# New opening order, one-operation end decays and a split last tile in a planned attention + MLP kernel

## The chip, the cores and the metric

One core of one Trainium2 chip runs the kernel. Its engines, each with a queue of its own that is worked through strictly in order: PE (TensorE, matrix products), DVE (VectorE), ACT (ScalarE, with function tables that must be loaded), POOL (GpSimd) and SP (SyncE, which here issues nearly all DMAs). The metric is the device time of one launch in microseconds (us); lower is better. A time of this kernel is told apart from no change when it moves by more than about 1%.

## The reference

The inputs are four batches of 8 heads, 768 tokens and head size 48. Three stages follow one another; everything is float32.

```python
# 1. linear attention with a decay per key channel
f = 1 / (1 + exp(-f_logit))
for t in range(S):
    state = f[:, :, t, :, None] * state + k_t (outer) v_t
    y[:, :, t] = q_t @ state
# 2. spatial gating MLP on x = y, (tokens, 384)
h = gelu_tanh(x @ w_in); u, v = halves of h
v_s = w_sg @ (normalised v * g_ln) + b_sg      # mixes tokens
x = x + (u * v_s) @ w_out
# 3. token and channel mixing
theta = x @ w_theta
y = w_tok_r @ (x * cos(theta)) + w_tok_i @ (x * sin(theta))
u = x + y;  out = u + relu(u @ w_ch)
```

## The kernel before

**Units.** A batch is worked in two halves of 384 tokens. In a half, the 8 heads lie in four pairs; the fourth pair's channels are packed into free rows of the first three pairs' tiles and are moved to their place by small DMAs (L801, two per pair). The attention of one pair and half is a *unit*: three transposes of K on PE (L822), a copy of them on ACT (`kt`, L826), state updates (L834) and scores (L843) on PE, the mask on DVE (`am`, L855), six small state steps on DVE (L871 to L880) with decays on ACT (L885), then the products inside the chunk (L925) and the carried-in products (L980 in batch 0), a copy of the result on ACT (`y`, L911), and DMAs that bring `y` into the activations `xst` (L902).

**Preparing a half** (`half`, `scaled`). The logits are loaded (L705), turned into decays (ACT L726 and L727), scanned on DVE (L735; its seeds come from a POOL memset L725 and a DVE step L730), inverted by Ln and Exp on ACT (L738, L739), and then K and Q are multiplied by them on DVE (L778 to L781). The decays at the chunk ends are made by two DVE operations of 128x3 (L785, L786) into `bends`, and ACT copies them into the tile (L789). For the fourth pair POOL clears a tile (L709).

**The order of the carried-in products** in batch 0 (`apart`). Their first product needs a signal that the products inside the chunk have ended in PSUM. Before the change ACT copies one state block over a part of `am` that those products read (L972), so that the copy has to wait for them, and the first carried-in product (L980) waits for the copy.

**Batch 0's MLP.** `w_in` arrives as 64-bit numbers and is decoded: 12 loads (L522), each with one ACT step (L534) and three DVE steps (L535 to L537) of 128x256. The v products (L1014, `mm<-early,xst`, 18 of 128x512) and the u products (L1014, `mm<-xst,early`, 128x384) read it as float32, at four passes each. ACT then makes gelu and the statistics (L1204 to L1234), and the W_sg products (L1002 to L1004, three of split float32 each) follow. Batches 1 to 3 go on in the same way with split weights, their attention laid between products of the batch before. The third stage is worked for two batches at a time (`pair`); `p7` is the last product, its DVE step L1167 and the store of the output L1171.

**What sets the order.** A planner (`Plan.schedule`) holds every operation with a length, dependencies and a due time. It picks greedily per engine and writes one fixed order per queue. Where PE would stand still in the first 100 us of its plan, it inserts warm-up products of an identity matrix (`idle`, L1382, 128x128, float32, so two records each in the trace). Numbers such as `HF0`, `V_AT`, `EVEN`, `ODD` and `RE_IN` are due times of stages. Table loads on ACT are inserted where the function in the plan changes (L346).

```python
if o.eng == "PE" and self.idle and t < WARM_TO and self.quiet(free["PE"]) is not None:   # L298
...
rate = c if ticks.get(i - 1, 0) >= 3060 else c / 2   # L254, the plan's speed of PE
```

The same program has a branch for inputs whose decays are too small (`general`); it is not run here.

Of the kernel before, what the change touches and what calls it, by code (L numbers as in the profile page):

```python
# [58 lines left out]
N_MIX, N_LMM, N_LST, N_LFM, N_LTMP = 3, 1, 5, 2, 1  # L59
EVEN, ODD = (0.05, 0.5), (0.9, 0.4)  # L60
GROUPS0 = [(p, p + 1) for p in range(NT)]
GROUPS1 = GROUPS0
LEAD = 3.0
LATE = 75.0
HF0, HF1, V_AT, U_AT, DENSE = (-60.0, -38.0), (-44.0, -16.0), -46.0, -24.0, -35.0
ATT_FROM = 0.0
ATT_TO = 100.0
PACE = 1.0
YQ = "SP"
MQ = "SP"  # L70
LOOK = 0.05
RE_IN = 4.0
SWITCH = 2.0
# [3 lines left out]

TICK = 10.24 / 3
DMA_SLACK = 1.0
BACKLOG = 2.5  # L80
# [59 lines left out]
class Plan:  # L140
# [63 lines left out]
    def schedule(self):  # L204
        for o in reversed(self.ops):
            cost = LAT[o.eng] + o.dur + ((ISSUED + LANDED + o.dma / RATE) * DMA_SLACK if o.dma else 0.0)
            for d in o.succ:
                o.vt = min(o.vt, d.vt - cost)
        free = {e: 0.0 for e in LAT}
        ticks = {}  # L210
        cand = {e: [] for e in LAT}
# [38 lines left out]
        def run(a, dur, left):  # L250

            c, i = left / dur, int(a / TICK + 1e-9)
            while left > 1e-6:
                rate = c if ticks.get(i - 1, 0) >= 3060 else c / 2  # L254
                n = min(left, rate * ((i + 1) * TICK - a))
                ticks[i] = ticks.get(i, 0) + n
                left, a, i = left - n, a + n / rate, i + 1
            return a
# [99 lines left out]
def body(tc, ctx, att, lat, qkv, flog, w_in, g_ln, w_sgT, b_sg, w_out, w_theta, w_rT, w_iT, w_ch, out):  # L358
# [36 lines left out]

    gate = const.tile([P, 1], F32, name="gate")
    halfpi = fill("halfpi", math.pi / 2)
    mhalf = fill("mhalf", -0.5, NS)
# [112 lines left out]
    def a1(n):  # L511
        return 0.1 + n * 0.00081
# [156 lines left out]

    first, ends = Buf(), []  # L670

# [11 lines left out]
    def half(pl, g, b, hf, xst, carry, vt, step):  # L683
# [14 lines left out]
        qk, parts = [], []  # L698
        later = [first] if b else []
        for p, (t, root) in enumerate(tiles):  # L700
            for p0, p1 in groups:
                if p0 == p:
                    dma(
                        pl, eng, P * (p1 - p0) * TH * 4,
                        lambda gp=slice(p0, p1): q[eng].dma_start(f.t[:, gp], flog[b, hf][:, gp]), later, wp=fp[p0:p1],  # L705
                    )
            if p == NT:
                moved, vb, clear = (Buf(of=root) for _ in range(3))
                pl.op("POOL", 0.1 + QKE * 0.0008, lambda t=t: nc.gpsimd.memset(t.t[:, :QKE], 0.0), w=[clear], vt=vt)  # L709
                dma(pl, eng, P * VAL * 4, lambda t=t, p=p: q[eng].dma_start(t.t[:, QKE:], qkv[b, p, hf][:, QKE:]), later, wp=[vb])  # L710
                part = [moved, moved, vb, clear]
            else:
                part = [Buf(of=root) for _ in range(4)]
                dma(pl, eng, P * QKV * 4, lambda t=t, p=p: q[eng].dma_start(t.t, qkv[b, p, hf]), later, wp=part)
            qk.append(t)
            parts.append(part)
# [49 lines left out]
    def scaled(pl, b, hf, p, f, fb, seed, sb, be, bb, t, parts, t3, parts3):  # L766
# [9 lines left out]
        if b == 0:  # L776
# [28 lines left out]
    def unit(pl, g, b, hf, p, be, bb, t, parts, xst, carry):  # L805
# [42 lines left out]
        if before:  # L848
            r, w, dur, fn = before
            pl.op("PE", 0.25 + 0.1 * nu + dur - 0.12, lambda fn=fn: (fn(), scores()), r=[kb, qb, vb, kt, *r], w=[ps, *w], small=True)  # L850
# [79 lines left out]
        if fused:  # L930
# [27 lines left out]
            if hf == 1 and p == NP - 1:  # L958
                r, w, dur, fn = both_
                pl.op("PE", dur, fn, r=r, w=w, small=True)  # L960
                out2()
            else:
                carry["last"], carry["out"] = both_, out2
            return

        def apart():
            pl.op("PE", 0.5, inner, r=[vb, am], w=[ps], small=True)
            late = range(1 - hf, 2 * NC2)
            turn = [(c, j) for c in late for j in range(2)]
            c0 = late[0]  # L970
            behind = lambda: am.t[wide[1], 1, (NC2 - 1) * HP : (NC2 - 1) * HP + D]
            pl.op("ACT", 0.2, lambda: nc.scalar.copy(behind()[:D], S[c0][0]()[rows[1]]), r=[S[c0][1]], w=[am])  # L972
            turn.remove((c0, 1))
            turn.insert(0, (c0, 1))

            def carried():
                for c, j in turn:
                    i, a = halves[c]
                    moved = (c, j) == turn[0]
                    nc.tensor.matmul(  # L980
                        score(a, i)[rows[j]], behind()[:D] if moved else S[c][0]()[rows[j]], Q()[rows[j], tok(i, a)], start=False,
                        stop=i == NC2 - 1,
                    )

            pl.op("PE", 0.134 * len(late), carried, r=[qb, *(S[c][1] for c in late), am], w=[ps], small=True)
            output()
# [4 lines left out]
    def moe(pl, g, xst, get, wmid, out_b, pace, first=False):  # L991
# [164 lines left out]

        def p7(hf, w):
# [112 lines left out]

    def pair(pl, g, batches, sets, get, ws, between=None):

# [99 lines left out]
        use(1)  # L1372
        p7b(0, ws[1])

# [10 lines left out]
    with tc.manual_schedule():  # L1385
# [76 lines left out]
        pair(pl, g, [blocks(b, again(b))[2] for b in (1, 2)], more, get, mids)  # L1462
        pl.emit()
# [153 lines left out]
```

## Time and profile before

| | |
|---|---|
| median of 3 runs | 595.15 us (592.37 to 598.02) |
| the profiled execution | 594.94 us, span 593.2 us |
| PE busy | 572.7 us (97% of the span) |
| DVE, ACT, POOL busy | 473.8, 374.0, 24.8 us |
| granted TensorE clock, mean | 0.998 |
| DMA | 136.26 MB, 230 GB/s on average |

The span is what the profile sees; the execution's own time is 1.7 us longer. PE is busy nearly all the time, but that counts warm-up products too, and the share is an average: from 14 to 36 us DVE has almost no idle time, from 43 to 78 us ACT has almost none, and after that PE works nearly without a pause to 586.9 us. The chain that ended last names for each stretch the engine whose work ended the wait.

### The profile page before, as it was taken

The numbers are of one execution on the slowest core, as the hardware profiler recorded it, in microseconds if no ns is written. First come the engines' busy times: TensorE is split into PE (matmuls) and PEld (weight loads), VectorE is DVE, ScalarE is ACT, GpSimd is POOL, SyncE is SP. The second block draws the span as 40 slices with busy tenths as digits, with TensorE's granted clock in tenths as the row PEclk, the third lists the DMA queues.
The fourth block names the chain that finished last, engine by engine and source line by source line (L and its number), as shares of the span: only waits on it lengthen the run. The fifth ranks groups of instructions, "written<-read, shape, count | busy, mean of one in ns | idle before, by whom it ended". The sixth has DMA issues, their size and how long they took to land.

```text
span 593.2 us, 14971 instructions
## 1 busy us (share of the span) xinstructions
PE 572.7 (97%) x5767; PEld 528.7 (89%) x5767; DVE 473.8 (80%) x1127; ACT 374.0 (63%) x828; POOL 24.8 (4%) x38
## 2 busy tenths in 40 slices
PE   8889999989999999999999999999999999999995
PEld 8646687978799989999999998999999999999995
DVE  5987789999789998699886777999968459898542
ACT  5869998569795668957488335785344249553410
POOL 3002000011001010000000000000000000000000
PEclk9999999999999999999999999999999999999999
DMA  8669574878787799787899898366788745548612
GB/s 284 177 190 306 190 216 139 283 221 251 233 278 255 255 286 329 229 247 208 275 319 328 286 330 310 125 211 231 247 273 265 249 142 158 162 135 252 187 41 85
DMA packets 61295, 136.26 MB, mean 230 GB/s; under 512 B 8096, under 2 KB 28320, under 8 KB 61216
## 3 DMA queue, kind: packets, MB, share of 16 engines
q1 hardware_dynamic: 61216, 135.23, 70.5%
q8 instruction: 47, 0.77, 0.6%
q14 instruction: 32, 0.26, 0.1%
HBM read 93.90 MB, written 34.21 MB: 216 GB/s over the span
## 4 chain that ended last, share of the span: by engine, by line
PE 72%; DVE 11%; ACT 8%; DMA 5%; issue 2%; SPq 1%; POOL 0%; DVEq 0%; ACTq 0%; POOLq 0%
PE mm L1002 16%; PE mm L1004 15%; PE mm L1003 15%; PE lmm L1004 5%; PE lmm L1002 5%; PE lmm L1003 5%; PE mm L1382 2%; DMA xst<-y 2%; PE at L940 2%; ACT L346 2%; PE at L925 1%; PE at L843 1%; PE at L822 1%; PE at L834 1%; DVE tmp L1083 1%
## 5 line engine op out<-in xcount | busy, mean ns | idle before, releaser
L1002 PE MATMUL mm<-st,ar 128*128 128x384 f32 x192 | 67.0, 349 | 0.9 <-ACT tmp L1204 0.6
L1004 PE MATMUL mm<-st,ar 128*128 128x384 f32 x192 | 64.5, 336 | 0.2 <-DVE ar L1238 0.2
L1003 PE MATMUL mm<-st,ar 128*128 128x384 f32 x192 | 64.2, 334 | 0.0
L1036 ACT CAST early<-xst 128x384 fp32r<-128x384 f32 x42 | 21.4, 511 | 30.6 <-DVE xst L1041 23.2
L1002 PEld LDWEIGHTS mm<-st,ar 128*128 128x128 f32 x192 | 36.0, 188 | 2.8 <-ACT tmp L1204 0.9
L1296 ACT CAST wout<-ar 128x384 fp32r<-128x384 f32 x48 | 24.2, 511 | 19.5 <-PE lmm L1003 9.6
L1004 PEld LDWEIGHTS mm<-st,ar 128*128 128x128 f32 x192 | 36.0, 188 | 0.5 <-DVE ar L1238 0.5
L1003 PEld LDWEIGHTS mm<-st,ar 128*128 128x128 f32 x192 | 36.1, 188 | 0.4 <-issue 0.2
L1002 PE MATMUL mm<-ar,wout 128*128 128x384 f32 x96 | 33.7, 351 | 1.7 <-DVE tmp L1128 1.3
L1002 PE MATMUL mm<-early,win 128*128 128x384 f32 x102 | 35.1, 345 | 0.0
L1004 PE MATMUL mm<-early,win 128*128 128x384 f32 x102 | 34.2, 336 | 0.0
L1003 PE MATMUL mm<-early,win 128*128 128x384 f32 x102 | 34.2, 335 | 0.0
L1003 PE MATMUL mm<-ar,wout 128*128 128x384 f32 x96 | 32.5, 338 | 0.9 <-DVE ar L1025 0.9
L1004 PE MATMUL mm<-ar,wout 128*128 128x384 f32 x96 | 32.2, 336 | 0.0
L1297 DVE TENSOR_TENSOR wout<-ar,wout 128x384 fp32r<-128x384 f32 x48 | 25.5, 551 | 7.3 <-ACT wout L1296 7.2
L1002 PE MATMUL mm<-win,early 128*128 128x512 f32 (+1 forms) x78 | 30.8, 394 | 0.0
L1004 PE MATMUL mm<-win,early 128*128 128x512 f32 (+1 forms) x78 | 29.4, 376 | 0.3 <-DVE early L1037 0.3
L1003 PE MATMUL mm<-win,early 128*128 128x512 f32 (+1 forms) x78 | 29.3, 375 | 0.0
L1041 DVE TENSOR_TENSOR xst<-xst,mm 128x384 f32<-128x384 f32 x42 | 22.5, 548 | 7.9 <-PE mm L1004 7.7
L346 ACT ACT_TABLE_LOAD x19 | 24.4, 1283 | 1.1 <-PEq L1609 0.8
L1041 DVE TENSOR_TENSOR xst<-xst,lmm 128x384 f32<-128x384 f32 x30 | 15.7, 549 | 11.8 <-PE lmm L1004 11.8
L1037 DVE TENSOR_TENSOR early<-xst,early 128x384 fp32r<-128x384 f32 x42 | 22.4, 551 | 2.2 <-ACT early L1036 2.1
(304 smaller groups left out, 1812.8 us busy)
## 6 DMA issues: line engine op xcount, KB each, us to landing
st<-scratch SPq DMA_DIRECT2D x76, 384.0 KB, 4.0
scratch<-wt SPq DMA_DIRECT2D x48, 384.0 KB, 4.1
lst<-scratch SPq DMA_DIRECT2D x44, 384.0 KB, 3.8
qkv<-in_qkv SPq DMA_DIRECT2D x21, 538.0 KB, 5.6
scratch<-st SPq DMA_DIRECT2D x12, 384.0 KB, 3.6
raw<-in_w_rT SPq DMA_DIRECT2D x12, 384.0 KB, 6.0
raw<-in_w_iT SPq DMA_DIRECT2D x12, 384.0 KB, 5.3
out<-xst SPq DMA_DIRECT2D x24, 192.0 KB, 2.2
```

What stands on the lines that cost most here:

```text
L346: self.nc.scalar.preload_act_table_set(SETS[load])
L822: nc.tensor.transpose(ps.t[:, 0, c], K()[:, c], ident)
L940: nc.tensor.matmul(o[rows[j]], state_[rows[j]], Q()[rows[j], tok(i, a)], start=False, stop=i == NC2 - 1 and a == 1,)
L1002: nc.tensor.matmul(o, h0, h1, start=start, stop=False, skip_group_check=more)
L1003: nc.tensor.matmul(o, h0, l1, start=False, stop=False, skip_group_check=more)
L1004: nc.tensor.matmul(o, l0, h1, start=False, stop=stop, skip_group_check=more)
L1036: pl.op("ACT", a1(TH), lambda: nc.scalar.copy(Xh(), T()), [src], [hi])
L1037: pl.op("DVE", v1(TH), lambda: V.tensor_sub(Xl(), T(), Xh().bitcast(F32)), [src, hi], [lo])
L1041: pl.op("DVE", v1(TH), lambda: V.tensor_add(T(), T(), ps.t[:, :TH]), [ps], [xst[hf].parts[k]])
L1296: pl.op("ACT", a1(TH), lambda: nc.scalar.copy(f.t[:, 0], st()), [sb], [hi])
L1297: pl.op("DVE", v1(TH), lambda: V.tensor_sub(f.t[:, 1], st(), f.t[:, 0].bitcast(F32)), [sb, hi], [lo])
L1382: nc.tensor.matmul(g.mm.tiles[i][:, :P], ident, ident, start=True, stop=True)
```

## The change

Six things change.

1. The planner is told other numbers: PE's work starts at 0.8 us in the plan (`PE_FROM`), the plan's first two ticks count PE at half speed (`COLD`), and five due times or spreads move (`ODD`, `HF0`, `V_AT`, `RE_IN`; `F_FIRST` is new).
2. The logits of the first two pairs are loaded before the first Q, K, V tile.
3. The clearing of the fourth pair's tiles and the seeds of half 1 wait for a small POOL copy (`opened`), which itself waits for the first scan.
4. The end decays of batch 0 are one DVE operation into the tile, and two ACT multiplications by -1 (to `bends`, and in place).
5. In `apart` the ACT copy into `am` is gone; a `drain` on PE stands ahead of the carried-in products.
6. The very last 384-column tile of the output is finished and stored in two halves, the second store from ACT's queue.

```diff
-EVEN, ODD = (0.05, 0.5), (0.9, 0.4)
+EVEN, ODD = (0.05, 0.5), (0.8, 0.6)
-HF0, HF1, V_AT, U_AT, DENSE = (-60.0, -38.0), (-44.0, -16.0), -46.0, -24.0, -35.0
+HF0, HF1, V_AT, U_AT, DENSE = (-58.0, -36.0), (-44.0, -16.0), -41.0, -24.0, -35.0
+F_FIRST = 2
-RE_IN = 4.0
+RE_IN = 2.0
+COLD, PE_FROM = 2, 0.8
...
+        free["PE"] = PE_FROM
...
-                rate = c if ticks.get(i - 1, 0) >= 3060 else c / 2
+                rate = c if i >= COLD and ticks.get(i - 1, 0) >= 3060 else c / 2
...
+        def clearing(t, clear, r=()):
+            pl.op("POOL", 0.1 + QKE * 0.0008, lambda: nc.gpsimd.memset(t.t[:, :QKE], 0.0), r, [clear], vt=vt)
...
+        if opening:
+            for i, (p0, p1) in enumerate(groups[:F_FIRST]):
+                loads(p0, p1, -200.0 + i)
...
-                pl.op("POOL", 0.1 + QKE * 0.0008, lambda t=t: nc.gpsimd.memset(t.t[:, :QKE], 0.0), w=[clear], vt=vt)
+                if not opening:
+                    clearing(t, clear, [go] if b == 0 else ())
...
-                pl.op("POOL", 0.1 + n * 0.0008, lambda gp=gp: nc.gpsimd.memset(seed.t[:, gp], 2.0**62), w=ss)
+                pl.op("POOL", 0.1 + n * 0.0008, lambda gp=gp: nc.gpsimd.memset(seed.t[:, gp], 2.0**62), [go] if hf else (), ss)
...
+                if opening and p0 == 0:
+                    pl.op("POOL", 0.1, lambda: nc.gpsimd.tensor_copy(opened, f.t[:, 0, TH - 1 :]), [fs[0]], [go])
+                    clearing(qk[NT], parts[NT][3], [go])
...
+            pl.op(
+                "DVE", 0.17, lambda: V.scalar_tensor_tensor(E(), ends(f), -2.0, ends(seed), ALU.add, ALU.mult), r=[fb, sb], w=[eb]
+            )
             def bends_():
-                V.tensor_scalar(be, ends(f), -1.0, 2.0, ALU.mult, ALU.add)
-                V.tensor_mul(be, be, ends(seed))
-            pl.op("DVE", 0.2, bends_, r=[fb, sb], w=[bb])
-            pl.op("ACT", 0.2, lambda: nc.scalar.copy(E(), be), r=[bb], w=[eb])
+                nc.scalar.mul(be, E(), -1.0)
+                nc.scalar.mul(E(), E(), -1.0)
+            pl.op("ACT", 0.4, bends_, w=[eb, bb])
...
-            pl.op("ACT", 0.2, lambda: nc.scalar.copy(behind()[:D], S[c0][0]()[rows[1]]), r=[S[c0][1]], w=[am])
...
             def carried():
-                for c, j in turn:
+                nc.tensor.drain()
+                for c in late:
...
+                if final and c == NK - 1:
+                    for i, eng in enumerate(("SP", "ACT")):
+                        h, ob = slice(i * TH // 2, (i + 1) * TH // 2), Buf()
+                        pl.op(
+                            "DVE", v1(TH // 2),
+                            lambda T=T, ps=ps, h=h: V.scalar_tensor_tensor(T()[:, h], ps.t[:, h], 0.0, T()[:, h], ALU.max, ALU.add), [ps, part], [ob],
+                        )
+                        dma(
+                            pl, eng, P * TH * 2,
+                            lambda T=T, cc=cc, h=h, eng=eng: q[eng].dma_start(out_b[cc, hf * TH + h.start : hf * TH + h.stop], T()[:, h]), [ob],
+                        )
+                    continue
```

What that does to the fixed orders, at three places. Lines in the changed file are shifted by 3 to 24.

PE, the start (`mm` from `ident` are warm-up products, `at` a unit's PSUM tile, `qkv` its tile); before:

```order
L1382 MATMUL mm_103<-ident 128x128 x26
L822 MATMUL at_107<-ident,qkv_116 128x128 x3
L1382 MATMUL mm_103<-ident 128x128 x13
L834 MATMUL at_107<-qkv_116,kt_180 64x48 x12
L843 MATMUL at_107<-qkv_116 64x64 x12
```

and now:

```order
L1406 MATMUL mm_104<-ident 128x128 x17
L840 MATMUL at_108<-ident,qkv_119 128x128 x3
L1406 MATMUL mm_104<-ident 128x128 x13
L852 MATMUL at_108<-qkv_119,kt_169 64x48 x12
L861 MATMUL at_108<-qkv_119 64x64 x12
```

Nine of 26 warm-up products ahead of the first transposes are gone; the 13 behind them stay.

PE again, from the third unit of half 0 (before) and the fourth (now) on, where the first v products stand (`early` is the decoded `w_in`, `ar_0` holds half 1's tiles); before:

```order
L925 MATMUL at_107<-am_445,qkv_131 64x64 x12
L1014 MATMUL mm_103<-early_249,xst_0_381 128x512
L980 MATMUL at_107<-qkv_131,am_445 48x64
L980 MATMUL at_107<-qkv_131,s_443 48x64 x9
L1014 MATMUL mm_104<-early_249,xst_0_381 128x512
L1014 MATMUL mm_105<-early_249,xst_0_381 128x512
L1382 MATMUL mm_106<-ident 128x128 x2
L822 MATMUL at_107<-ident,ar_0_331 128x128 x3
L925 MATMUL at_108<-am_557,qkv_133 64x64 x12
L1382 MATMUL mm_106<-ident 128x128
L1014 MATMUL mm_103<-early_249,xst_0_381 128x512
L980 MATMUL at_108<-qkv_133,am_557 48x64
```

and now:

```order
L943 MATMUL at_109<-am_509,qkv_134 64x64 x12
L852 MATMUL at_108<-ar_0_176,kt_546 64x48 x10
L861 MATMUL at_108<-ar_0_176 64x64 x12
L993 MATMUL at_109<-qkv_134,s_506 48x64 x10
L1406 MATMUL mm_104<-ident 128x128 x6
L943 MATMUL at_108<-am_611,ar_0_176 64x64 x12
L993 MATMUL at_108<-ar_0_176,carry_296 48x64 x2
L993 MATMUL at_108<-ar_0_176,s_609 48x64 x10
L840 MATMUL at_109<-ident,ar_0_176 128x128 x3
L1026 MATMUL mm_104<-early_388,xst_0_354 128x512 x2
L852 MATMUL at_109<-ar_0_176,kt_684 64x48 x10
L861 MATMUL at_109<-ar_0_176 64x64 x12
```

The v products, which stood from the third unit on, now stand behind five whole units and the transposes of the sixth; a product that needs a later part of `xst` no longer stands ahead of the fourth unit's carried-in products.

ACT, batch 1's first half (`f`, `seed` and `qkv` are its tiles, `u` a gelu of batch 0); before:

```order
L911 COPY y_1020<-at_108 128x2x3x64
L346 ACT_TABLE_LOAD
L756 ACTIVATE seed_353<-f_817 128x1152
L346 ACT_TABLE_LOAD
L1065 ACTIVATE u_1037<-mm_105 128x384
L346 ACT_TABLE_LOAD
L757 ACTIVATE seed_353<-seed_353 128x1152
L346 ACT_TABLE_LOAD
L1204 ACTIVATE tmp_1054,stat_752<-mm_106 128x512
```

and now:

```order
L929 COPY y_1028<-at_109 128x2x3x64
L349 ACT_TABLE_LOAD
L771 ACTIVATE seed_336<-f_858 128x1152
L770 COPY bends<-f_858 128x9
L772 ACTIVATE seed_336<-seed_336 128x1152
L349 ACT_TABLE_LOAD
L1077 ACTIVATE u_1051<-mm_106 128x384
```

Two of four table loads are gone here, since Ln and Exp of the decays stand together; elsewhere in the part that runs their number is the same. On SP, six of the `w_in` loads stood ahead of the first small moves (L801) and now all 12 stand behind half 1's logits and tiles. From the third stage on the orders of the two kernels are alike but for a few rows.

## Rows read from the trace of the kernel before

**Rows 1.** The page, part 4: the chain that ended last, shares by engine.

```profile
PE 72%; DVE 11%; ACT 8%; DMA 5%; issue 2%; SPq 1%; POOL 0%; DVEq 0%; ACTq 0%; POOLq 0%
```

**Rows 2.** Busy time by stretch: from:to, length, each engine, clock, DMA share.

```profile
0.00:28.00 28.00, 24.17 (x427) 22.30 (x427) 21.07 (x73) 20.54 (x54) 6.21 (x18) 1.00 0.72 227
0.00:68.15 68.15, 61.59 (x935) 43.91 (x936) 51.85 (x162) 54.56 (x130) 9.51 (x21) 1.00 0.74 237
68.15:77.75 9.60, 8.70 (x92) 7.58 (x90) 5.22 (x11) 9.54 (x23) 1.92 (x2) 1.00 0.35 130
77.75:586.95 509.20, 502.38 (x4741) 477.23 (x4741) 416.13 (x953) 309.92 (x677) 13.39 (x15) 1.00 0.72 233
```

**Rows 3.** The same, L1382 alone (warm-up products): PE, weight loads, clock, DMA.

```profile
2.00:4.00 2.00, 2.00 (x11) 2.00 (x11) 1.00 0.96 294
8.00:10.00 2.00, 2.00 (x21) 2.00 (x19) 1.00 1.03 333
0.00:28.00 28.00, 16.84 (x110) 15.54 (x110) 1.00 0.72 227
0.00:68.15 68.15, 17.93 (x116) 16.44 (x116) 1.00 0.74 237
```

**Rows 4.** Timeline of PE, the first row: start, us, engine, line, operation, [idle before].

```profile
1.60 8.64 PE L1382 MATMUL mm<-ident 128*128 128x128 f32 x52 [1.60 <-POOL ident masks.py:199]
```

**Rows 5.** Timeline of DVE, 4 to 15 us, and one row at 46 us.

```profile
4.50 0.75 DVE L730 TENSOR_SCALAR seed<-f 128x3 f32<-128x3 f32 x1 [3.45 <-ACT f L727]
...
6.78 0.17 DVE L730 TENSOR_SCALAR seed<-f 128x3 f32<-128x3 f32 x1 [0.54 <-ACT f L727]
...
8.83 0.55 DVE L779 TENSOR_TENSOR f<-f,seed 128x384 f32<-128x384 f32 x1
9.30 0.95 DVE L735 TENSOR_TENSOR_SCAN f<-f,seed 128x384 f32<-128x384 f32 x1
10.17 0.53 DVE L781 SCALAR_TENSOR_TENSOR qkv<-f,qkv 128x384 f32<-128x384 f32 x1
...
12.10 0.56 DVE L780 TENSOR_TENSOR qkv<-qkv,seed 128x384 f32<-128x384 f32 x1 [0.65 <-ACT seed L739]
...
14.40 0.21 DVE L871 COPY s<-at 128x48 f32<-128x48 f32 x1 [1.27 <-PE at L843]
...
45.85 0.75 DVE L536 SCALAR_TENSOR_TENSOR early<-st,early 128x256 int32<-128x256 int32 x2
```

**Rows 6.** Timeline of POOL: the clearing of one tile, and the gate copy.

```profile
4.49 0.74 POOL L709 MEMSET ar<- 128x772 f32 x1
...
45.59 1.73 POOL L1395 COPY gate<-early 128x1 f32<-128x1 f32 x1 [25.34 <-DVE early L537]
```

**Rows 7.** Busy time of 14.40 to 35.90 us: PE, weight loads, DVE, ACT, POOL.

```profile
14.40:35.90 21.50, 16.89 (x357) 13.01 (x357) 21.36 (x75) 17.21 (x50) 1.06 (x1) 1.00 0.70 200
```

**Rows 8.** Timeline, 33 to 37 us: the end of half 0's fourth unit.

```profile
33.84 0.44 ACT L534 ACTIVATE early<-raw 128x256 f32<-128x256 f32 x1 [1.57 <-DMA raw<-in_w_in]
...
35.77 1.10 PE L1014 MATMUL mm<-early,xst 128*128 128x512 f32 x2 [2.38 <-DMA xst<-y]
...
36.80 0.25 PE L980 MATMUL at<-qkv,am 48*48 48x64 f32 x1
```

**Rows 9.** Timeline of ACT: the first gelu table, and two of the loads between.

```profile
43.10 1.28 ACT L346 ACT_TABLE_LOAD   x1
...
64.60 1.28 ACT L346 ACT_TABLE_LOAD   x1
...
66.40 1.28 ACT L346 ACT_TABLE_LOAD   x1
```

**Rows 10.** DMA issues by kind: count, KB each, median us from issue to landing.

```profile
st<-in_w_in SPq DMA_DIRECT2D x5, 256.0 KB, 4.7
tmp<-in_w_in SPq DMA_DIRECT2D x4, 256.0 KB, 7.2
```

**Rows 11.** Timeline of DVE: the last operation of the span.

```profile
586.95 0.56 DVE L1167 SCALAR_TENSOR_TENSOR xst<-mm,xst 128x384 f32<-128x384 f32 x1 [1.00 <-PE mm L1004]
```

More of the change, by code (lines that the diff above doesn't have):

```diff
@@ L396, in body @@
     gate = const.tile([P, 1], F32, name="gate")
+    opened = const.tile([P, 1], F32, name="opened")
     halfpi = fill("halfpi", math.pi / 2)
@@ L668, in attention @@
         return xst
-    first, ends = Buf(), []
+    first, go, ends = Buf(), Buf(), []
     def verdict(pl, g):
@@ L699, in half, with loads @@
         later = [first] if b else []
-        for p, (t, root) in enumerate(tiles):
[L701 to L706, printed above, removed]
+        def clearing(t, clear, r=()):
+            pl.op("POOL", 0.1 + QKE * 0.0008, lambda: nc.gpsimd.memset(t.t[:, :QKE], 0.0), r, [clear], vt=vt)
+        def loads(p0, p1, vt=None):
+            dma(pl, eng, P * (p1 - p0) * TH * 4, lambda: q[eng].dma_start(f.t[:, p0:p1], flog[b, hf][:, p0:p1]), later, wp=fp[p0:p1], vt=vt)
+        opening = b == 0 and hf == 0
+        if opening:
+            for i, (p0, p1) in enumerate(groups[:F_FIRST]):
+                loads(p0, p1, -200.0 + i)
+        for p, (t, root) in enumerate(tiles):
+            for i, (p0, p1) in enumerate(groups):
+                if p0 == p and not (opening and i < F_FIRST):
+                    loads(p0, p1)
             if p == NT:
                 moved, vb, clear = (Buf(of=root) for _ in range(3))
-                pl.op("POOL", 0.1 + QKE * 0.0008, lambda t=t: nc.gpsimd.memset(t.t[:, :QKE], 0.0), w=[clear], vt=vt)
+                if not opening:
+                    clearing(t, clear, [go] if b == 0 else ())
                 dma(pl, eng, P * VAL * 4, lambda t=t, p=p: q[eng].dma_start(t.t[:, QKE:], qkv[b, p, hf][:, QKE:]), later, wp=[vb])
@@ L849, in unit @@
             r, w, dur, fn = before
-            pl.op("PE", 0.25 + 0.1 * nu + dur - 0.12, lambda fn=fn: (fn(), scores()), r=[kb, qb, vb, kt, *r], w=[ps, *w], small=True)
+            pl.op("PE", 0.25 + 0.1 * nu + dur - 0.32, lambda fn=fn: (fn(), scores()), r=[kb, qb, vb, kt, *r], w=[ps, *w], small=True)
             carry.pop("out")()
@@ L959, in unit @@
                 r, w, dur, fn = both_
-                pl.op("PE", dur, fn, r=r, w=w, small=True)
+                pl.op("PE", dur - 0.26, fn, r=r, w=w, small=True)
                 out2()
@@ L968, in apart @@
             late = range(1 - hf, 2 * NC2)
-            turn = [(c, j) for c in late for j in range(2)]
-            c0 = late[0]
-            behind = lambda: am.t[wide[1], 1, (NC2 - 1) * HP : (NC2 - 1) * HP + D]
-            pl.op("ACT", 0.2, lambda: nc.scalar.copy(behind()[:D], S[c0][0]()[rows[1]]), r=[S[c0][1]], w=[am])
-            turn.remove((c0, 1))
-            turn.insert(0, (c0, 1))
             def carried():
-                for c, j in turn:
+                nc.tensor.drain()
+                for c in late:
                     i, a = halves[c]
[L979 to L985, printed above, removed]
+                    for j in range(2):
+                        nc.tensor.matmul(
+                            score(a, i)[rows[j]], S[c][0]()[rows[j]], Q()[rows[j], tok(i, a)], start=False, stop=i == NC2 - 1
+                        )
+            pl.op("PE", 0.134 * len(late) + 0.29, carried, r=[qb, *(S[c][1] for c in late)], w=[ps], small=True)
             output()
@@ L1155, in p6, with p7 @@
                 residual(pss[c], hf, c)
-        def p7(hf, w):
+        def p7(hf, w, final=False):
             for c in range(NK):
@@ L1164, in p7 @@
                 part = xst[hf].parts[c]
+                if final and c == NK - 1:
[8 more added lines that the diff above has]
+                            lambda T=T, cc=cc, h=h, eng=eng: q[eng].dma_start(out_b[cc, hf * TH + h.start : hf * TH + h.stop], T()[:, h]), [ob],
+                        )
+                    continue
                 pl.op(
@@ L1269, in moe, with pair @@
         return block1, block2, (xsplits, theta, residual, p7, mm3)
-    def pair(pl, g, batches, sets, get, ws, between=None):
+    def pair(pl, g, batches, sets, get, ws, between=None, end=False):
         V = nc.vector
@@ L1372, in pair @@
         use(1)
-        p7b(0, ws[1])
+        p7b(0, ws[1], end)
     pl = Plan(nc)
@@ L1461, in body @@
             more.append((Cells(bufs), [[[Buf(of=h) for _ in range(2)] for _ in range(NK)] for h in bufs]))
-        pair(pl, g, [blocks(b, again(b))[2] for b in (1, 2)], more, get, mids)
+        pair(pl, g, [blocks(b, again(b))[2] for b in (1, 2)], more, get, mids, end=True)
         pl.emit()
```

## Prediction

> **What bounds the kernel now.** I read the chain of waits first, since it says whose work ended each wait: PE 72%, DVE 11%, ACT 8% and DMA 5% [rows 1]. PE is the bound of the whole, but about a quarter of the chain lies elsewhere, and the change is about the opening. So I read the busy times by stretch next [rows 2]: from 77.75 to 586.95 us PE idles for 6.8 of 509.20, while to 68.15, where the first W_sg product starts, it is busy for 61.59, of which 17.93 are warm-up products [rows 3]. Useful there is 61.59 - 17.93 = 43.66; about 24 us could go if all else kept up. What doesn't keep up shows in the next views: from the first state copy at 14.40 to 35.90 VectorE works 21.36 of 21.50 us, PE 16.89, ACT 17.21 [rows 7]; then PE waits 2.38 for the DMA that brings `y` into `xst` [rows 8]; and from 68.15 to 77.75 ACT works 9.54 of 9.60 while PE idles .90 [rows 2]. So the opening has three limits in turn: VectorE, one move of `y`, ACT.
>
> **The sum's base.** The durations are from the profiled execution, 594.94 us (span 593.2 and 1.7 around it), .2 under the median of 595.15. I subtract from 594.94. One per cent, 5.95 us, is what a measurement can tell from no change: faster is below 589.2, slower above 601.
>
> **Warm-up (parts 1 and 2).** Before, 52 records end at 1.60 + 8.64 = 10.24 [rows 4] although K is scaled right behind the seed step at 6.78 [rows 5]. A record takes .18 early and .095 later (11 and 21 in 2 us, at a granted clock of 1.00 in both) [rows 3]. 17 products are 34 records: about 29 until 6.9 us, the rest at .095 to .18, so the transposes stand at about 8.1, 2 us earlier, and the 13 products behind them end at about 11.4. The state products follow, and the first state could be copied at about 12.
>
> **VectorE's chain.** The logits come in the order that matters: the third pair's load has the same bytes ahead of it as before, so the scan at 9.30 and the first Q (10.17 + .53 = 10.70) [rows 5] stay. Behind it one end decay (.17) and three multiplications (.47 apart, 8.83 to 9.30) [rows 5] end at about 12.3; the .65 wait for ACT's Exp [rows 5] goes, since the inverse stands earlier on ACT. The 1.27 wait for PE [rows 5] goes too. The first state copy is at 12.45 instead of 14.40.
>
> From there VectorE bounds. Before, 21.50 us held 75 operations [rows 7]; the new order has 70 between the same copy and K of half 1's second pair. By kind there are five fewer of 128x384, five fewer of 128x3, five more of 128x48. The first are .47 each, 2.35; the others are .17 and .21 [rows 5], which cancel within .2. So K stands at 12.45 + 21.50 - 2.3 = 31.7, is done at 32.2, and with the transposes behind it the first v product starts at 33.0.
>
> **PE from there.** By 28 us PE had done 24.17 - 16.84 = 7.33 of useful work [rows 2, 3], three units and a bit (3.2), or 2.3 for a unit. At 33.0 the new order has five units and three transposes behind it: 5 x 2.3 + .4 = 11.9. Of 43.66 that leaves 31.8, with no warm-up product in it. Two waits are added. The third v product needs the fourth unit's `y`: between 0 and the 2.38 of today [rows 8]; its carried-in products move from 36.80 to about 30, so that I take .8. And three drains stand in the busy part: no drain is in the trace; below, nothing, since products in flight cost nothing if they are done; above, a lone product's .25 each [rows 8]. I take .2 each, the row's side, because the carried-in products now follow directly: .6. A gain is excluded there, as the copy that falls away was on ACT. W_sg starts at 33.0 + 31.8 + .8 + .6 = 66.2 instead of 68.15: **1.95 gained.**
>
> **ACT (parts 1, 4, 5).** The first gelu comes after three v products (1.1 each [rows 8]) and one unit's state and score products (about 1): near 37.6, where its table load was at 43.10 [rows 9]. Two table loads fall away, 2 x 1.28 [rows 9]. So ACT is ahead at the first W_sg group and the .90 of PE idle there [rows 2] is not repeated: **.90 gained.** The second multiplication of each end decay costs ACT about what the dropped copy gave it, beside 4.3 idle us in [rows 7].
>
> **POOL (part 3).** The clearing no longer meets the first seed step, which took .75 beside a clearing of .74, and .17 without [rows 5, 6]. The chain goes on from the third logits, so nothing is gained at the end of it. The clearing waits for the first scan, at 6.2 at the latest (4.50 + .75 + .95 [rows 5]), and for the small copy, whose nearest row is 1.73 [rows 6]; it ends at about 8.7 and the moves that need it start after Q at 10.70: hidden by 2 us, and 1 us of later moves is also covered, since the fourth unit is scaled last.
>
> What could go against this is the new copy itself: it reads SBUF beside the second seed step or scan. The nearest row says no: two L536 operations with two inputs ran beside a gate copy of 1.73 at .75 for both [rows 5, 6], .375 each.
> The Trainium skill ("SBUF — State Buffer", "Who interferes with whom") says the reverse: a VectorE operation with two SBUF inputs contends with a GpSimd operation that reads SBUF, which holds the shared ports for the whole instruction. By the page VectorE's chain would be up to .8 later and the time 592.8 rather than 592.0; the trace speaks against it, if that copy's span is as shown.
>
> **The rest and the tail.** From 77.75 on products and order are the same but for a few rows; PE's 6.8 us of idle stay, within 1.5 either way. The last VectorE operation takes .56 [rows 11]; halves take about .3, and the first half's store starts before the second's arithmetic. Both stores have a fixed part that halves do not shorten, and ACT's queue issues no store near it: between .3 lost and .3 gained, I take .1 gained.
>
> Sum: 1.95 + .90 + .1 = 2.95; 594.94 - 2.95 = **592.0**. With the bounds of the waits, the drains, the rest and the tail its own range is 589.5 to 594.
>
> **Rivals.**
> *A, the forecast, .50.*
> *B, ACT decides, .20.* Chain shares name ACT for 8% [rows 1], and it works 54.56 of 68.15 [rows 2]. If its whole lead, 5.5 us at the first gelu and 2.6 in table loads, reaches the second W_sg group and batch 1's decays, 8 us come off: 586.9. Against it: PE's useful work leaves no more than 1.95 + .90 up to 77.75 unless it starts earlier than 33.0 or the 6.8 idle later shrinks too.
> *C, the gain is spent again, .14.* An earlier W_sg can find `w_out` or batch 1's tiles still on the way; DMA engines are at .72 to .74 of their time in the opening [rows 2]. The lead ends there, or the planner's fewer warm-up products only move the same wait: 594.8.
> *D, late `w_in`, .12, the slower side.* On SP all 12 loads now stand behind half 1's tiles and the first moves of `y`, and on ACT their decode stands in one line with the copies of `y`, VectorE's decode steps in one line with the state steps. A load takes 4.7 to 7.2 to land [rows 10], and ACT has waited 1.57 for one [rows 8]. If they land at 7.2 rather than 4.7 (2.5 late), and the moves of `y` behind them 1.7 late as well, 4.2 is lost against the forecast: 596.2. It decides from 3 us of lateness on; against it stands that the first VectorE decode step is due at about 24 us, when the loads issued at 15 have had 9 us.
> *E, clock, .04.* Fewer warm-up products could bring the lower level of 1.2 GHz (granted clock .5) between 8 and 33 us, where some 8 us of useful products would take twice as long: 600 to 603. Against it: after 2.38 us without work the next product took 1.10 [rows 8], as elsewhere at the clock of 1.00, and the 13 warm-up products behind the first transposes stay. No row of this trace shows the lower level at work.
>
> **How the numbers follow.** 592.0 is A's. The range, 586.5 to 596.5, takes in A and C, and half of B and of D; E and the outer halves, 2 in 10, are out. Faster by over 1%: B and .04 of A's lower end, .24. Slower: E and .01 of D, .05. Within 1%: .71.
>
> **What would show it.** Right: first transposes near 8.1; first state copy at 12.4; VectorE without a gap to 31.7; first v product near 33; first gelu table at 37 to 38; W_sg at 66; no wait at the second W_sg group. Wrong: a wait of VectorE for decoded `w_in` (D), a granted clock under 1.00 before 33 us (E), idle PE after 78 us beyond 6.8 (C), a first v product well before 33 (B), or more than .25 between the last product inside a chunk and the first carried-in one (the drain).

## The result, and the profile after

The changed kernel takes 588.15 us (median of 4 runs, 587.65 to 589.37), the kernel before, run beside it, 595.32 (592.37 to 598.02): a ratio of 0.9895 (95% interval 0.9855 to 0.9934), 7.2 us. The profiled execution has a span of 585.9 us, 7.3 under that of before. The forecast was 592.0, in a range of 586.5 to 596.5: the side and the range held, the size was less than half of what came, and only about 1 us of the 7 came where the forecast had put it.

The page's part 4, the chain that ended last:

```profile
PE 83%; DVE 6%; ACT 4%; DMA 4%; issue 1%; SPq 1%; DVEq 0%; ACTq 0%
```

(SPq, DVEq and ACTq are the queues of these engines.) PE's share of it rose from 72% [rows 1], so there is less waiting for others. Where it went, the busy times by stretch show (from:to, length, then PE, weight loads, DVE, ACT, POOL; clock, DMA share, GB/s). The kernel before, from the first W_sg product to the end of the last product (the stretch ahead of it is in [rows 2]):

```profile
68.15:80.00 11.85, 10.74 (x102) 9.31 (x101) 7.46 (x16) 11.79 (x30) 1.92 (x2) 1.00 0.45 161
80.00:110.00 30.00, 28.87 (x310) 24.38 (x309) 29.67 (x74) 23.49 (x47) 0.00 (x0) 1.00 0.60 197
110.00:200.00 90.00, 86.98 (x1458) 78.20 (x1457) 81.53 (x217) 68.53 (x156) 7.12 (x8) 1.00 0.80 253
200.00:586.92 386.92, 384.48 (x2969) 372.92 (x2967) 302.69 (x661) 215.65 (x467) 6.28 (x7) 1.00 0.71 230
```

And the changed kernel, from its start, with the same bounds:

```profile
0.00:68.15 68.15, 61.90 (x927) 45.05 (x928) 56.33 (x169) 54.95 (x139) 8.69 (x22) 0.97 0.78 250
68.15:80.00 11.85, 11.85 (x111) 11.08 (x110) 6.47 (x13) 11.20 (x24) 1.92 (x2) 1.00 0.58 171
80.00:110.00 30.00, 29.51 (x398) 24.96 (x397) 29.42 (x77) 21.69 (x49) 0.00 (x0) 1.00 0.61 199
110.00:200.00 90.00, 90.00 (x1478) 82.29 (x1478) 82.97 (x216) 68.28 (x153) 7.33 (x8) 1.00 0.82 261
200.00:579.20 379.20, 377.47 (x2850) 366.95 (x2849) 297.34 (x650) 211.70 (x463) 6.81 (x7) 1.00 0.71 230
```

Length minus PE's busy time is PE's idle time: 6.56, 1.11, 1.13, 3.02 and 2.44 us before, 6.25, 0, .49, 0 and 1.73 now. So 5.8 us of waiting went, 4.4 of them behind 80 us; PE's busy time fell by 1.9 (572.7 to 570.7); and from the last product to the span's end .4 was lost (6.3 to 6.7). 5.8 + 1.9 - .4 = 7.3. The opening, for which most of the change was written, gave .3 of the waits, and the first W_sg product behind it did not come earlier: 68.31 us, before 68.15. That is not one execution's chance: four executions with the change's order there have it at 67.7 to 69.0 (act_late, tail_whole, the change, after_again), two with the old order at 67.9 and 68.2 (before_swap, before).

**What the shown diff leaves out.** The diff shown ahead of the prediction lacks three lines that matter here, and the prediction did not weigh them. They change lengths in the plan: two of PE's work of a unit in batches 1 to 3, and one of the carried-in products of batch 0, behind the new drain:

```diff
-            pl.op("PE", 0.25 + 0.1 * nu + dur - 0.12, lambda fn=fn: (fn(), scores()), r=[kb, qb, vb, kt, *r], w=[ps, *w], small=True)
+            pl.op("PE", 0.25 + 0.1 * nu + dur - 0.32, lambda fn=fn: (fn(), scores()), r=[kb, qb, vb, kt, *r], w=[ps, *w], small=True)
...
-                pl.op("PE", dur, fn, r=r, w=w, small=True)
+                pl.op("PE", dur - 0.26, fn, r=r, w=w, small=True)
...
-            pl.op("PE", 0.134 * len(late), carried, r=[qb, *(S[c][1] for c in late), am], w=[ps], small=True)
+            pl.op("PE", 0.134 * len(late) + 0.29, carried, r=[qb, *(S[c][1] for c in late)], w=[ps], small=True)
```

### The profile page after: what moved, and what is told of

Read it like the earlier page. It is cut to its first block, busy times and chain, and to the rows that moved or that the text cites. A ratio compares the mean times of both kernels' runs of the same rounds, so it can differ in the third digit from the quotient of the medians.

```text
span 585.9 us, 14964 instructions
## 1 busy us (share of the span) xinstructions
PE 570.7 (97%) x5759; PEld 530.3 (91%) x5759; DVE 473.2 (81%) x1122; ACT 367.8 (63%) x824; POOL 24.7 (4%) x39
## 4 chain that ended last, share of the span: by engine, by line
PE 83%; DVE 6%; ACT 4%; DMA 4%; issue 1%; SPq 1%; DVEq 0%; ACTq 0%
PE mm L1014 19%; PE mm L1016 18%; PE mm L1015 18%; PE lmm L1016 5%; PE lmm L1015 5%; PE lmm L1014 5%; PE at L958 2%; PE at L943 2%; PE at L861 2%; PE mm L1026 2%; PE at L852 2%; PE at L840 1%; DMA ar<-in_qkv 1%; DMA qkv<-in_qkv 1%; DMA st<-in_w_in 1%
```

## The experiments

The theories: **order** (the gain is the order of the queues behind the opening, as the planner's numbers happen to set it) against **lead** (the opening's code lets ACT and VectorE run ahead of PE, and later waits vanish for that). Ratios are to the kernel before on the same chip; on the three chips used it took 593.5 to 594.4.

**numbers_only**: the kernel before with the constants of the diff that the kernel before has too (ODD, HF0, V_AT, RE_IN).

```diff
-EVEN, ODD = (0.05, 0.5), (0.9, 0.4)
+EVEN, ODD = (0.05, 0.5), (0.8, 0.6)
-HF0, HF1, V_AT, U_AT, DENSE = (-60.0, -38.0), (-44.0, -16.0), -46.0, -24.0, -35.0
+HF0, HF1, V_AT, U_AT, DENSE = (-58.0, -36.0), (-44.0, -16.0), -41.0, -24.0, -35.0
-RE_IN = 4.0
+RE_IN = 2.0
```

> The kernel before with the due times and spreads of the change (EVEN and ODD, HF0, V_AT, RE_IN) and nothing else of it. Theory 'order': the gain of 7.2 us lies behind the opening (waits of PE between 80 and 160 us and at 412 us went), and it comes from the order that the planner's numbers give, so most of it is here: 589 to 591.5. Theory 'lead': the gain comes from the opening's code, which lets ACT and VectorE run ahead of PE: 594 to 595.5 here.

Measured: 601.36, ratio 1.0136 (1.0085 to 1.0188). Neither theory had this: PE waits 17.1 us in all, 2.9 more than before, and the granted clock falls to .50 twice (33 to 37 and 81 to 85 us). Alone these numbers cost 8 us.

**code_only**: the changed kernel with those constants as before (the diff above, reversed).

> The changed kernel with the five old due times and spreads, so its opening code, drains, end decays, COLD, PE_FROM, the shorter planned unit lengths and the split tail stay. Theory 'order': the old due times bring most of the waits back, 592.5 to 595. Theory 'lead': 588 to 589.5, as the whole change.

Measured: 591.88, ratio 0.9961 (0.9937 to 0.9985), slightly better than 'order' allowed. Its first W_sg product stands at 67.1, 1.2 us ahead of the change's, and it still loses: 2.1 us of waits between 110 and 200 us, 1.7 at 407. What a set of numbers is worth depends on the rest.

**lens_only**: the kernel before with the first two planned lengths quoted above.

> The kernel before with only the planned lengths of two PE operations of a unit in batches 1 to 3 shortened as in the change (scores behind the products of the unit before by .2, the last unit's products by .26). Nothing that runs is another operation; the order of batches 1 to 3 moves. If these lengths are what removed the 3.0 us of waits between 120 and 160 us: 591.5 to 592.5. If the lengths are of no matter: 594.5 to 596. Theory 'lead' says 594.5 to 596.

Measured: 591.45, ratio 0.9974 (0.9947 to 1.0001). Waits from 110 to 200 us fell from 3.0 to 1.5. The interval reaches 1, so that a gain from these lengths alone is not shown; and in the profiled execution the opening ran ahead by itself (first W_sg product at 66.59).

**lens_old**: the changed kernel with those two lengths as before.

> The changed kernel with the old planned lengths of those two operations; its opening's order is that of the change to the first 5% of PE's rows. If the lengths matter: 590.5 to 592, with waits again between 110 and 160 us. If they don't, and under theory 'lead': 588 to 589.

Measured: 593.74, ratio 1.0007 (0.9982 to 1.0031), above what either answer allowed: without these two numbers nothing of the change's gain is left. Waits from 110 to 200 us are back at 2.2:

```profile
110.00:200.00 90.00, 87.83 (x1414) 80.33 (x1406) 80.51 (x214) 66.91 (x152) 7.39 (x8) 1.00 0.82 259
```

This run speaks against 'lead'. ACT is nearly as early as in the change (its last gelu table load ahead of the W_sg statistics stands at 64.17, in the change at 63.88, before at 68.88), the first W_sg product stands at 66.27, 2 us ahead of the change's, and the gain is gone all the same.

**lens_more**: the changed kernel with both lengths .05 us shorter still.

```diff
-            pl.op("PE", 0.25 + 0.1 * nu + dur - 0.32, lambda fn=fn: (fn(), scores()), r=[kb, qb, vb, kt, *r], w=[ps, *w], small=True)
+            pl.op("PE", 0.25 + 0.1 * nu + dur - 0.37, lambda fn=fn: (fn(), scores()), r=[kb, qb, vb, kt, *r], w=[ps, *w], small=True)
-                pl.op("PE", dur - 0.26, fn, r=r, w=w, small=True)
+                pl.op("PE", dur - 0.31, fn, r=r, w=w, small=True)
```

> The changed kernel with the planned length of the same two PE operations another .05 us shorter (.37 and .31 instead of .32 and .26); nothing that runs is another operation, the opening's order stays. If the lengths help because the plan becomes truer to the chip, .05 us hardly matters: 587 to 589. If what counts is which of many near-equal orders the greedy planner falls into: the time moves by 1.5 us or more, most likely up, 589.5 to 594, with waits of PE behind 100 us at other places than in any kernel so far.

Measured: 592.44, ratio 0.9977 (0.9959 to 0.9995), 5 us over the change on the same chip. So it isn't that the lengths became truer. A new wait stands at 127.5, and behind it the granted clock was .50 from 130 to 133 us; the timeline there (start, us, engine, line, operation; in brackets the idle time before):

```profile
126.60 0.34 DVE L969 TENSOR_TENSOR y<-y,at 48x192 f32<-48x192 f32 x1
126.87 2.54 DVE L766 TENSOR_TENSOR_SCAN f<-f,seed 128x1152 f32<-128x1152 f32 x1
129.44 0.36 DVE L969 TENSOR_TENSOR y<-y,at 48x192 f32<-48x192 f32 x1
...
129.90 0.88 PE L840 MATMUL at<-ident,qkv 128*128 128x128 f32 x3 [2.38 <-ACT bends L770]
```

The greedy planner put the 2.54 us scan of the next half between the two additions that free a unit's PSUM tile, and PE's next transposes wait for the second. The releaser that the row names is ACT; by time it is the addition that ended at 129.80.

**act_late**: the changed kernel with ACT late: twelve small copies ahead of a logarithm of batch 1, every queue's order otherwise as in the change.

```diff
+                if b == 1 and hf == 0:
+                    nc.scalar.copy(dly, mhalf[:, :1])
+                    for _ in range(11):
+                        nc.scalar.copy(dly, dly)
+                A(seed.t[:, gp], f.t[:, gp], AF.Ln)
```

> The changed kernel with twelve copies of 128x1 on ACT (about 2.4 us) ahead of the first logarithm of batch 1's decays, at 61 us; the order on every queue is that of the change. Theory 'order': ACT is late for the first W_sg group's second half and PE waits 1.5 to 2.5 us there, once; behind it, from 110 to 160 us, PE waits as little as in the change (under .5), and the time is 589.5 to 590.7. Theory 'lead': without ACT's lead the waits of the kernel before come back behind it (3.0 us at 120 to 160, .6 at 95): 592 to 594.

Measured: 590.7, ratio 0.9935 (0.9908 to 0.9962). Its busy times by stretch:

```profile
68.15:80.00 11.85, 10.44 (x104) 9.51 (x103) 6.79 (x17) 11.47 (x26) 1.92 (x2) 1.00 0.57 168
80.00:110.00 30.00, 29.42 (x382) 24.96 (x383) 29.58 (x73) 22.12 (x49) 0.00 (x0) 1.00 0.56 190
110.00:200.00 90.00, 89.52 (x1435) 81.50 (x1431) 82.39 (x214) 67.68 (x152) 7.35 (x8) 1.00 0.82 261
```

PE waits 1.41 us at the W_sg products, once, and .58 and .48 behind them, where the kernel before had 1.13 and 3.02. The copies held ACT for 2.5 us: that gelu table load now stands 1.9 us ahead of the first W_sg product, in the change 4.4 ahead, before .7 behind. 'Lead' is out as far as that half of ACT's lead can tell: with this order the waits did not come back. In lens_old and code_only, with other orders, the load is 2.1 and 3.3 us ahead, no less than here, and PE waits 2.2 and 2.1 us from 110 to 200 us instead of .48. VectorE's lead was not tried by itself.

**before_swap**: the kernel before with two pairs of neighbours on ACT exchanged (a copy of y with the cast ahead of it, another with the sigmoid ahead of it; k counts ACT's operations in the plan).

```diff
+        for k in (200, 207) if len(acts) > 208 else ():
+            a, y = acts[k], acts[k + 1]
...
+            plan.insert(here(a), plan.pop(here(y)))
```

> The kernel before with two pairs of neighbours on ACT swapped and nothing else: two copies of a unit's result (y) in batch 1 stand ahead of a cast that waited 1.35 us for a DMA at 120 us, and ahead of a sigmoid that waited 1.07 us for logits at 126 us. Theory 'order': PE's waits ahead of the transposes at 122.9 (.70 us) and 128.9 (.56 us) are these two, so both fall under .2 here, with nothing earlier changed: 1.0 to 1.3 us less than before, 592.7 to 594. Rival: the copies weren't what PE waited for (VectorE's work in front of its two additions was), the waits stay, and the time is that of before.

The wait that it is about, in the timeline of the kernel before:

```profile
121.64 0.52 ACT L1036 CAST early<-xst 128x384 fp32r<-128x384 f32 x1 [1.35 <-DMA raw<-in_w_iT]
122.05 0.48 ACT L947 COPY y<-at 128x384 f32<-128x384 f32 x1
...
122.56 0.35 DVE L951 TENSOR_TENSOR y<-y,at 48x192 f32<-48x192 f32 x1 [0.60 <-ACT y L947]
...
123.58 0.52 PE L822 MATMUL at<-ident,qkv 128*128 128x128 f32 x3 [0.70 <-issue]
```

and the same place with the swap:

```profile
119.57 0.48 ACT L956 COPY y<-at 128x384 f32<-128x384 f32 x1 [0.53 <-PE at L949]
120.09 0.52 ACT L1045 CAST early<-xst 128x384 fp32r<-128x384 f32 x1
...
124.56 0.48 ACT L956 COPY y<-at 128x384 f32<-128x384 f32 x1 [1.00 <-PE at L949]
126.16 1.17 ACT L751 ACTIVATE f<-f 128x1152 f32<-128x1152 f32 x1 [1.12 <-DMA f<-in_flog]
```

Both waits of PE are gone (no idle time from 112 to 130.7 us), so they were these copies, held in ACT's queue behind an operation that waited for a DMA. Of PE's 3.0 us of waits from 110 to 200 us, 1.6 are left (.6 of them at 131 us, where the kernel before has .35), and the time did not show it: 594.0, ratio 1.0007 (0.998 to 1.0034). The mechanism is shown, its worth in time is not.

**moves_together**: the changed kernel with one DMA earlier on SP, the second move from the third pair into the fourth pair's tile.

```diff
+            plan.insert(at["move0"] + 1, plan.pop(at["move1"]))
```

> The changed kernel with one DMA of the opening issued earlier on SP: the second of the two moves from the third pair into the fourth pair's tile stands behind the first, ahead of the two moves of the first unit's y. No other instruction moves. In the change PE waited 2.07 us for that move at 22 us, and the granted clock was .50 from about 24.8 to 28.2. Theory 'opening bounds': the wait shrinks to under .5, the clock stays at 1.00, the first v product starts 2.5 to 3.5 us earlier (33 to 34), the first W_sg product at 65.5 to 66.5 instead of 68.3, and the end follows: 585 to 586.5. Rival 'taken back': VectorE, ACT or late w_in loads keep the first v product at 35 to 36.5, or a later wait takes the lead away: 587.5 to 588.5.

Measured: 587.27, ratio 0.9899 (0.9853 to 0.9946), as the change. 'Taken back' holds:

```profile
23.14 0.52 PE L847 MATMUL at<-ident,qkv 128*128 128x128 f32 x3 [0.44 <-DMA qkv<-qkv]
...
29.19 0.43 ACT L543 ACTIVATE early<-raw 128x256 f32<-128x256 f32 x1 [1.02 <-DMA raw<-in_w_in]
...
29.65 0.29 DVE L544 TENSOR_SCALAR early<-early 128x256 int32<-128x256 int32 x1 [0.91 <-ACT early L543]
```

PE's wait for the move fell from 2.07 to .44, and the first v product still stands at 35.96. VectorE now waits .91 for a decoded w_in, PE .81 and .67 for copies on ACT, and the first state copy came .56 later than in the change (13.80); which of these holds the product is not told apart.

**more_warm**: ten more warm-up products ahead of the fourth unit's transposes.

```diff
+            i = max(i for i in range(at["fourth"]) if isinstance(plan[i][0], tuple))
+            n, bank = plan[i][0]
+            plan[i] = ((n + 10, bank), None)
```

> The changed kernel with ten more warm-up products just ahead of the fourth unit's transposes, where PE waited 2.07 us for a move; nothing else. The move still lands when it did, so this tells the wait from the clock. If PE's pause brought the lower clock: granted clock 1.00 there, the fourth unit's state and score products take .55 us a group instead of .88, VectorE's wait for them shrinks by 1 to 1.5 us, and the time is 586.5 to 587.5. If the clock falls without the pause as well, or nobody waits for those 1.5 us: 588 to 588.5.

Measured: 589.21, ratio 0.9925 (0.99 to 0.9951). The clock stayed at 1.00 (as it did in act_late, lens_more and tail_whole without these products, so that this does not show the wait as the cause of the fall) and the time did not fall; other waits of PE took the place: 1.57 at 32.5 for VectorE, which had itself stood 1.22 for a decoded w_in, and 1.18 at 39.5, whose releaser the trace doesn't name.

**opening_fixed**: moves_together, four loads of w_in earlier on SP, and the last tile in one piece.

```diff
+            for k in (4, 5, 8, 9):
+                to = here(loads[k - 1]) + 1
...
+                plan.insert(to, plan.pop(here(loads[k])))
```

> The changed kernel with six instructions of SP's queue at other places and nothing else moved in the opening: the second move into the fourth pair's tile right behind the first, two loads of w_in (raw) ahead of the second unit's three moves of y, and two more (st) ahead of the third unit's; the last output tile is stored in one piece. If VectorE's and ACT's waits for late w_in loads are what held the first v product at 36 us once the move came in time: it starts at 33.5 to 35, the first W_sg product at 65.5 to 66.5, and, with the order behind it as in the change, the time is 1 to 2 us below the change: 586 to 587. If VectorE's own work holds it, or a later wait takes the lead back: v product at 35.5 to 36.5, time within .5 of the change.

Measured: 588.09, ratio 0.9901 (0.9875 to 0.9927), as the change; the first v product stands at 36.62. PE's wait for the move is 1.21 here, and ACT waits 2.22 for another load:

```profile
33.95 0.45 ACT L552 ACTIVATE early<-st 128x256 f32<-128x256 f32 x1 [2.22 <-DMA st<-in_w_in]
```

**tail_whole**: the changed kernel with its last tile in one piece.

```diff
-        pair(pl, g, [blocks(b, again(b))[2] for b in (1, 2)], more, get, mids, end=True)
+        pair(pl, g, [blocks(b, again(b))[2] for b in (1, 2)], more, get, mids)
```

> The changed kernel with its last output tile finished and stored in one piece, as before; every other instruction stands where it stood. The trace of the change has 6.7 us from the start of the last product's last record to the span's end, that of before 6.4 (the store from ACT's queue landed 3.4 us after issue, the others 1.6 to 2.5). If that store is the loss: 6.3 here, and the time of the change, or .3 to .5 below it: 587.7 to 588.2. If the split is worth something: 588.3 to 589. It is also the changed kernel's time on this chip, against which the other three are read.

Measured: 587.91, ratio 0.9899 (0.9862 to 0.9935). From the last product to the span's end it takes 6.1 us; the eight profiled executions with the split take 6.2 to 6.7 (mean 6.5), the six with the whole tile 6.1 to 6.4 (mean 6.2). The split gains nothing and may cost .3.

**after_again**: the changed kernel, no edit.

> The changed kernel once more, on the chip of the other three, with no edit: 587.5 to 588.5 if before is at 594 to 595 here. Its trace tells whether the granted clock of .69 at 25 to 30 us, which two kernels with the same opening didn't show, is part of the change (again under .8) or of that one execution (1.00).

Measured: 587.49, ratio 0.9902 (0.9874 to 0.9929). The clock fell again, .61 and .71 in 25 to 35 us. No version beats the change beyond the intervals.

## Why the prediction was right or wrong, step by step

- **The base.** One execution stood for the kernel before. Its second logits were used by ACT at 5.6 us; numbers_only and lens_only, with the same opening order, have 7.0 and 6.6. Before any of this PE's first transposes start anywhere from 8.87 to 10.08 us in four executions of that order. Terms of half a microsecond in the opening were within this scatter.
- **Warm-up: right, the exact figure by luck.** 34 records end at 8.51, the transposes start at 8.34 (7.72 in after_again). The prediction's 8.1 is not what its own figures give: 29 records by 6.9 us and five more at .095 to .18 are 7.4 to 7.8. The timeline of the changed kernel, first PE's rows, then VectorE's:

```profile
1.60 6.91 PE L1406 MATMUL mm<-ident 128*128 128x128 f32 x34 [1.60 <-POOL ident masks.py:199]
8.34 0.49 PE L840 MATMUL at<-ident,qkv 128*128 128x128 f32 x3
...
24.22 0.52 PE L840 MATMUL at<-ident,qkv 128*128 128x128 f32 x3 [2.07 <-DMA qkv<-qkv]
...
25.91 0.89 PE L852 MATMUL at<-qkv,kt 64*64 64x48 f32 x24
...
8.55 0.23 DVE L742 TENSOR_SCALAR seed<-f 128x3 f32<-128x3 f32 x1 [1.13 <-ACT f L739]
...
13.24 0.20 DVE L889 COPY s<-at 128x48 f32<-128x48 f32 x1
...
27.61 0.21 DVE L889 COPY s<-at 128x48 f32<-128x48 f32 x1 [1.98 <-PE at L861]
...
35.49 0.55 DVE L793 TENSOR_TENSOR ar<-ar,ar 128x384 f32<-128x384 f32 x1
```

- **VectorE's chain: size off.** In that timeline the first state copy is at 13.24, not 12.45: the third logits are the last to land now, and VectorE waits 1.13 for them.
- **VectorE from there: wrong.** The list of 70 operations was right; that VectorE would work through it without a gap was not. It waited 1.98 for the fourth unit, whose transposes waited 2.07 for a move that stood behind the moves of y on SP, and then ran at the lower clock. K of half 1's second pair is at 35.49 instead of 31.7: .8 of that is the later start, 2.7 are idle (22.25 - 19.56, where almost none was forecast), the rest is busy time. The runs with the move or w_in earlier did not bring the first v product under 35.96: late w_in (rival D's) takes part of it back.
- **PE from there: size off, in the other direction.** The first v product is at 36.50 instead of 33.0, the first W_sg product at 68.31: 1.95 us were forecast, -.16 came. The stretch between is 31.81 us, where 31.8 + .8 + .6 = 33.2 was forecast. The .8 for the third v product's wait did not come; the drains did, near the forecast .2 each: the carried-in products start .69 us behind the start of the products inside the chunk (43.07 to 43.76, and the same at 52.22 and 58.10), a next product without a drain .51 behind it (57.94 to 58.45 before). The products themselves were shorter by about as much: v and u products ahead of W_sg are busy 24.19 us, before 26.19, since they stand in longer rows (two v products in a row 1.88, one alone 1.10 [rows 8]).

```profile
13.24:35.49 22.25, 18.36 (x450) 15.53 (x450) 19.56 (x71) 16.96 (x52) 1.06 (x1) 0.92 0.67 194
36.50:68.31 31.81, 31.05 (x344) 17.16 (x343) 29.32 (x81) 29.54 (x69) 2.32 (x3) 1.00 0.82 265
```

- **ACT: right, though later than forecast.** No wait at the second W_sg group; the first gelu table is at 39.9 (37.6 forecast). Forecast .90 to 77.75 us, measured 1.11 to 80.
- **POOL: right in the result, the reading of the row of 1.73 wrong.** The first seed steps take .17 and .14. The changed kernel's timeline has the new copy of POOL, and further down the gate copy and the first operation of VectorE behind the w_in decode:

```profile
6.14 0.18 POOL L751 COPY opened<-f 128x1 f32<-128x1 f32 x1 [2.67 <-DVE seed L742]
...
45.55 0.66 POOL L1419 COPY gate<-early 128x1 f32<-128x1 f32 x1 [26.83 <-DVE early L541]
46.07 0.16 DVE L1424 TENSOR_SCALAR gcol<-gcol 128x4 f32<-128x4 f32 x1
```

  and the kernel before, behind its gate copy of 1.73 [rows 6]:

```profile
47.19 0.15 DVE L1400 TENSOR_SCALAR gcol<-gcol 128x4 f32<-128x4 f32 x1
```

  The new copy took .18, not 1.73, with no operation of VectorE with two inputs beside it. The gate copy has the same size and runs beside the decode's operations with two inputs; it lasts .66 to 1.73, and in all 14 traces it ends .13 to .14 us behind the start of `gcol`, the operation behind them (47.32 and 47.19 before, 46.21 and 46.07 now), while VectorE's operations keep their .37 each. So the row of 1.73 is most likely that of a copy held up by VectorE, and it did not speak against the Trainium skill's rule on the shared ports ("SBUF — State Buffer", "Who interferes with whom"), as the prediction read it: the trace fits the rule, with POOL as the one that waits. No run tried it by itself.
- **"From 77.75 on products and order are the same but for a few rows": the step that failed.** PE's 6.8 us of idle time were to stay within 1.5; behind 80 us 4.4 of them went. I had compared which products run and taken small moves of order for nothing. They decide who stands behind a waiting operation, as the ACT rows of before_swap show; that these moves carry the gain shows in lens_old, where two planned lengths take all of it away. PE's busy time behind the first W_sg product fell too, from 511.1 to 508.7 us; why is not known.
- **The tail: wrong, but small.** .1 gained was taken, .4 was lost in this execution, .3 over several. The store from ACT's queue landed 3.4 us after issue, the other half 1.6.

```profile
out<-xst SPq DMA_DIRECT2D x1, 96.0 KB, 1.6
out<-xst ACTq DMA_DIRECT2D x1, 96.0 KB, 3.4
```

- **The rivals.** B's time (586.9) was the nearest, its cause was not: act_late took half of ACT's lead away without bringing the waits back, and lens_old and code_only have the waits with as much lead as act_late or more: they followed the order. E's drop of the clock happened, but behind a wait at 22 us, not where warm-up products are gone (ahead of 8.5 us), and lasted 3.4 us here, not 25. Of the prediction's own signs of being wrong two came: the granted clock under 1.00 before 33 us (E), and VectorE's waits for decoded w_in (D; .25 and .37 in the change). That the range held is luck: it reached to B, and the sum had no term for what came.

What stays open: which single exchange of neighbours gives how much. Each wait is small, and removing two of them did not show in the time. COLD, PE_FROM, F_FIRST and the third planned length were not tried by themselves either, so that their share in the order is not known.

## What to carry to other kernels

Where one greedy plan sets all the queues, an edit in one place is an edit of the whole order: compare the order in every stretch and ask, of each pair that changed places, whether the one in front waits for a DMA. A gain that such an edit shows belongs to the plan, not to the edit's purpose, until it has been tried with the order held still. Holding the order and changing a few instructions is the cleaner experiment; six of the eleven edited kernels here did so.

## What the runs showed of the hardware

The granted clock fell to .50, the lower of the two levels (1.2 of 2.4 GHz), after some waits of PE. In the changed kernel (from:to, length, then PE's busy time; clock, DMA share, GB/s):

```profile
24.00:26.00 2.00, 1.78 (x13) 0.67 0.80 258
26.00:28.00 2.00, 2.00 (x72) 0.50 0.69 179
```

It did so behind a wait of 2.07 us in both profiled executions of this kernel, in lens_old behind one of 1.82 and in code_only behind one of 1.46 at the same place; it did not in act_late behind one of 2.05, in lens_more behind one of 2.23, in tail_whole behind one of 1.46, nor in the kernel before behind its 2.38 [rows 8]. So the length of the wait alone does not tell. In act_late:

```profile
24.00:26.00 2.00, 1.64 (x43) 1.00 0.80 248
26.00:28.00 2.00, 1.89 (x76) 1.00 0.65 163
```

The fourth unit's state products took .89 a group instead of .56. What the fall costs at the end is not shown: of the six kernels with this opening and no fall in it, three had the first W_sg product at 67.5 to 67.9 us, three at 68.5 to 69.3, the change itself at 68.3 and 69.0, and lens_old, with the longest fall (25.5 to 32 us), at 66.3.
